# A list scheduler inside the kernel decides the order in which five engines get their instructions

## The chip, the cores and the metric

The kernel runs on one core of one Trainium2 chip. The metric is the device time of one execution in microseconds (us); lower is better. Before the change the median of three runs was 364.27 us (362.97 to 366.21). PE is TensorE, DVE is VectorE, ACT is ScalarE, POOL is GpSimd, SP is SyncE, which here only issues DMAs; PEld in the profiles is the loading of weights into PE. The order in which the program emits the instructions is what this change is about: an instruction that has to wait holds up those behind it on its engine, as a stall of 4.39 us on ScalarE further down shows.

## The reference, cut to what matters

Two stages follow each other. The first is attention over 4 batches x 8 heads x 768 positions x 64 dimensions, in which every query may look at only the 6 best of its 32-key chunks. "Best" is an upper bound, computed from the per-chunk minima and maxima of the keys. The second is a gated FFN over the 3072 resulting rows.

```python
k_min = np.min(k_chunks, axis=3)                # chunks of 32 keys
k_max = np.max(k_chunks, axis=3)
ub = np.sum(np.maximum(q * k_min, q * k_max), axis=-1)      # shapes cut
top_chunks = np.argsort(ub, axis=-1)[..., -top_k:]          # top_k = 6, causal
scores = scale * np.matmul(q, k.transpose(0, 1, 3, 2))
scores = np.where(sel & causal, scores, -1e9)
attn = softmax(scores) @ v                                  # written out in full there
# x: 3072 rows of 512, width of the FFN 1536
xn = x / rms(x) * rms_g
out = (silu(xn @ w_gate) * (xn @ w_val)) @ w_out
```

## The kernel before

The work falls into 12 blocks of 256 tokens. For each block and each group of four heads ("job") there is a preparation: transpose k and q (`kT`, `qT`), cast them (`kb`, `qb`), cast v (`VX`), place the chunk bounds (`KS`), compute the upper bounds on PE (`ub`), rank them and turn them into masks (`mt`, and `mo`, a copy of `mt` on the other half of the partitions). Then come the score units (`sc`, exponentials `pt`), the values (`avn`), the normalised rows (`xnat`, scaled `xs`, turned `tp`/`xsT`), and the FFN: six pairs of gate and value matmuls (`gp`, `vp`) and two projections (`op`) per block.

The values of a job are cast by GpSimd:

```python
def p_values(j):
    nc.gpsimd.tensor_copy(VX[j % KEEP_K][:, :, :, 0:D], st[j]["vraw"][:])
```

The order of all this is a fixed interleave, written by hand. The first two blocks have a script of their own (cut). After that a loop over the score units puts one slice of FFN and one step of preparation between the parts of a unit:

```python
for i in range(2, NU):
    ...
    if nxt:
        need(nxt)
        scores(nxt)
    sl = next_slice(i, 0)          # a gate/value pair or a projection, if due
    sl and sl.part()
    if nxt:
        exps(nxt, 0)
        triangle(nxt, 0)
    prep(0)                        # one step of a later job's preparation
    sl and sl.part()
    if nxt:
        exps(nxt, 1)
        triangle(nxt, 1)
    sl and sl.rest()
    run_later()
    ...
    values(u, 0, avn, [kg], pts)
    if last:
        normalise(u, 0, avn)
    prep(1)
    sl = next_slice(i, 1)
    sl and sl.rest()
    ...
```

The softmax here doesn't subtract the row's maximum and nothing guards it: scores larger than these inputs give would overflow.

## Time and profile before

| | before |
|---|---|
| median time | 364.27 us (3 runs) |
| span of the profiled run | 364.5 us |
| PE busy / idle | 316.9 / 47.6 us |
| mean granted clock of PE | 0.934 |
| first gate matmul of the FFN | 33.5 us |

These are lines of the profile's page: busy times by engine, then the lines of PE, VectorE and the clock that cut the span into 40 slices of 9.1 us (a digit is the busy share in tenths; `PEclk` is the granted clock in tenths), and the chain of work that ended last.

```profile
span 364.5 us, 11291 instructions
...
PE 316.9 (87%) x4565; PEld 230.6 (63%) x4588; DVE 233.5 (64%) x583; ACT 199.3 (55%) x321; POOL 197.1 (54%) x329
...
PE   8667987699779889899879889899799898998995
...
DVE  6676775657865875974875974876866946415240
...
PEclk9965998959996999999989989999989999999999
...
PE 56%; DVE 18%; DMA 8%; SPq 6%; ACT 5%; issue 5%; POOL 1%; DVEq 0%; POOLq 0%; ACTq 0%
...
```

PE is the engine that bounds the kernel, but it is not full in most slices, and its clock sags in the first third. The chain of waits goes through PE for 56% of the span and through VectorE for 18%. What PE waits for is in the view of waits (line, releaser, total us, times, longest):

```profile
...
PE sc L333 <- DVE mt L291: 11.8, 10, 2.1
PE tp L428 <- DVE xs L414: 6.3, 6, 2.8
PE avn L371 <- DVE xnat L386: 4.8, 6, 1.7
PE sc L333 <- DVE mo L297: 3.5, 10, 0.6
...
```

The next view gives the busy time of each engine in two stretches: up to the first gate matmul (at 33.5 us), then up to the last values of attention (at 328.6 us); the FFN that is left after that is not shown.

```profile
...
core 0: us, PE busy (x) PEld busy (x) DVE busy (x) ACT busy (x) POOL busy (x), PEclk, DMA share, GB/s
0.00:33.50 33.50, 23.12 (x246) 11.72 (x250) 21.90 (x66) 9.54 (x15) 19.13 (x45) 0.81 1.00 197
33.50:328.60 295.10, 263.18 (x4089) 196.72 (x4107) 200.91 (x502) 173.16 (x276) 163.22 (x270) 0.94 0.29 78
...
```

Read the last columns: the clock is 0.81 in the start and 0.94 in the long middle, and the DMA engines are full (share 1.00) only in the start. In the middle PE is idle for 295.1 - 263.2 = 31.9 us.

I also charged every matmul in the trace's records with the time until the next one starts, less the recorded idle time, and took off what the recorded half clock cost. That splits PE's time into real work at full clock, keep-warm matmuls (on zeros, to hold the clock up), clock loss, and idle. This split is worked out from the records of the profiled run, so its tenths are not to be pressed:

| before, us | real work | warm | clock loss | idle |
|---|---|---|---|---|
| 0 to 33.5 | 6.8 | 11.9 | 4.4 | 9.1 |
| 33.5 to 328.6 | 246.9 | 0 | 16.3 | 31.9 |
| 328.6 to 360.5 | 30.6 | 0 | 0 | 1.3 |

The 1.3 us before the first matmul and the last 4 us, for the final eviction and store, are outside the table. The profiled run was the slowest of the four of this kernel (366.21 us, clock 0.934); in the later rounds the clock of its runs is 0.934 to 0.950, with a median of 0.946. So some 4 us of the clock loss in this table may be this one run's: an estimate, (0.946 - 0.934) x 364.5.

### The profile page before, as it was taken

What the parts mean: (1) busy time and instruction counts of PE and PEld (TensorE: products, weight loads), DVE (VectorE), ACT (ScalarE), POOL (GpSimd) and SP (SyncE); (2) the same over time, 40 slices, a digit from 0 to 9 for tenths busy, and PEclk for the clock granted to TensorE, in tenths of its full rate; (3) what the DMA queues carried; (4) which work ended last, traced back from release to release, by engine and by line L of the source; (5) the groups of instructions that cost most, each with busy time, mean ns of one, the idle gap of its engine ahead of it and who ended that gap; (6) DMA issues with size and microseconds to landing.
All of it is one profiled execution on the core that took longest, in us unless ns stands there. A gap on an engine that the chain in (4) does not pass through costs nothing.

```text
span 364.5 us, 11291 instructions
## 1 busy us (share of the span) xinstructions
PE 316.9 (87%) x4565; PEld 230.6 (63%) x4588; DVE 233.5 (64%) x583; ACT 199.3 (55%) x321; POOL 197.1 (54%) x329
## 2 busy tenths in 40 slices
PE   8667987699779889899879889899799898998995
PEld 3334773478547657677756766777576675867682
DVE  6676775657865875974875974876866946415240
ACT  2340772537543754756554655775666475846361
POOL 6652592337844663763953752875763753336261
PEclk9965998959996999999989989999989999999999
DMA  6999954651242034125204204111001001010001
GB/s 178 191 198 241 220 148 134 174 131 43 66 141 70 20 88 121 42 74 147 72 18 147 64 27 146 45 39 67 3 2 59 2 3 59 2 46 17 30 31 58
DMA packets 43317, 30.63 MB, mean 84 GB/s; under 512 B 29440, under 2 KB 34048, under 8 KB 43264
## 3 DMA queue, kind: packets, MB, share of 16 engines
q1 hardware_dynamic: 38160, 24.66, 24.5%
q0 software_dynamic: 4720, 4.72, 7.9%
q8 instruction: 36, 0.59, 0.6%
q10 hardware_dynamic: 384, 0.52, 0.4%
q14 instruction: 17, 0.14, 0.1%
HBM read 28.31 MB, written 6.29 MB: 95 GB/s over the span
## 4 chain that ended last, share of the span: by engine, by line
PE 56%; DVE 18%; DMA 8%; SPq 6%; ACT 5%; issue 5%; POOL 1%; DVEq 0%; POOLq 0%; ACTq 0%
PE op L474 15%; PE gp L451 14%; PE vp L451 11%; DMA kraw<-in_k_dram 5%; PE ub L259 5%; PE avn L371 4%; SPq L88 4%; DVE tg L464 4%; PE sc L317 4%; ACT th L458 2%; DVE qT L197 2%; DVE xs L414 2%; PE sc L333 2%; DVE xnat L386 2%; DMA rmsg<-in_moe_rms_g_dram 2%
## 5 line engine op out<-in xcount | busy, mean ns | idle before, releaser
L468 POOL TENSOR_TENSOR hh<-tg,vs 128x512 bf16<-128x512 bf16 x72 | 83.0, 1153 | 70.6 <-ACT vs L461 55.5
L347 ACT ACTIVATE pt<-sc 128x768 bf16<-128x768 f32 (+1 forms) x96 | 85.6, 913 | 48.1 <-PE sc L333 48.0
L464 DVE SCALAR_TENSOR_TENSOR tg<-th,gp 128x512 bf16<-128x512 bf16 x72 | 49.2, 683 | 57.5 <-ACT th L458 55.7
L451 PE MATMUL gp<-xsT,wg 128*128 128x256 bf16 x576 | 80.0, 285 | 3.4 <-DVE xsT L430 2.0
L451 PE MATMUL vp<-xsT,wv 128*128 128x256 bf16 x576 | 79.6, 284 | 2.8 <-DVE tg L464 2.4
L474 PE MATMUL op<-wo,hh 128*128 128x512 bf16 x268 | 65.2, 387 | 2.0 <-issue 1.3
L451 PEld LDWEIGHTS <-wv 128*128 128x128 bf16 x576 | 58.7, 102 | 12.8 <-issue 3.7
L451 PEld LDWEIGHTS <-wg 128*128 128x128 bf16 x576 | 53.8, 101 | 15.4 <-issue 5.4
L458 ACT ACTIVATE th<-gp 128x512 bf16<-128x512 f32 x72 | 43.1, 598 | 30.3 <-PE gp L451 26.9
L461 ACT ACTIVATE vs<-vp 128x512 bf16<-128x512 f32 x72 | 43.2, 600 | 15.3 <-PE vp L451 13.8
L474 PEld LDWEIGHTS <-hh 128*128 128x128 bf16 x288 | 26.6, 99 | 33.3 <-issue 3.1
L481 ACT ACTIVATE osb<-op 128x512 f32<-128x512 f32 x24 | 14.3, 597 | 47.5 <-PE op L474 46.3
L371 PEld LDWEIGHTS <-pt 128*128 128x128 bf16 x672 | 31.0, 101 | 13.4 <-DVE xnat L386 6.5
L333 PE MATMUL sc<-mt,chunkrow 32*128 32x128 bf16 (+1 forms) x352 | 27.1, 213 | 11.8 <-DVE mt L291 11.8
L317 PE MATMUL sc<-qb,kb 32*128 32x256 bf16 (+1 forms) x768 | 36.0, 266 | 1.5 <-DVE ubn L270 1.5
L355 POOL TENSOR_SCALAR_AFFINE_SELECT pt<-pt 128x512 bf16<-128x512 bf16 x48 | 30.6, 640 | 9.0 <-ACT pt L347 7.8
L333 PEld LDWEIGHTS <-chunkrow 32*128 32x128 bf16 x704 | 20.3, 96 | 20.0 <-issue 18.9
L197 DVE STREAM_TRANSPOSE qT<-qraw 128x512 f32<-128x512 f32 x24 | 26.6, 1106 | 0.6
L270 DVE STREAM_TRANSPOSE ubn<-ub 128x256 f32<-128x256 f32 (+1 forms) x24 | 9.2, 381 | 27.5 <-PE ub L259 27.2
L197 DVE STREAM_TRANSPOSE kT<-kraw 128x512 f32<-128x512 f32 x24 | 26.5, 1104 | 0.1
L333 PE MATMUL sc<-mo,chunkrow 32*128 32x128 bf16 (+1 forms) x352 | 23.0, 214 | 3.5 <-DVE mo L297 3.5
L234 POOL TENSOR_SCALAR qraw<-qT 128x512 f32<-128x512 f32 (+1 forms) x24 | 12.5, 519 | 21.0 <-DVE qT L197 18.3
(138 smaller groups left out, 389.4 us busy)
## 6 DMA issues: line engine op xcount, KB each, us to landing
vraw<-in_v_dram SPq DMA_DIRECT2D x48, 128.0 KB, 2.9
out_dram<-osb SPq DMA_DIRECT2D x24, 256.0 KB, 2.1
kraw<-in_k_dram SPq DMA_DIRECT2D x92, 64.0 KB, 2.3
qraw<-in_q_dram SPq DMA_DIRECT2D x92, 64.0 KB, 2.0
wg<-in_moe_w_gate_dram POOLq DMA_DIRECT2D x3, 512.0 KB, 7.3
wv<-in_moe_w_val_dram POOLq DMA_DIRECT2D x3, 512.0 KB, 10.1
wo<-in_moe_w_out_dram POOLq DMA_DIRECT2D x1, 1536.0 KB, 19.3
kraw<-in_k_dram ACTq DMA_DIRECT2D x4, 64.0 KB, 2.4
```

Source lines behind the costliest of these rows:

```text
L197: nc.vector.transpose(out=st[j][nm + "T"].rearrange("p h (r j) -> p j h r", r=32, j=8), in_=st[j][nm + "raw"][:],)
L317: nc.tensor.matmul(sc[a // 2][:, a % 2, 256 * e:256 * e + BLK - q0], st[jk]["kb"][r, t, ks], st[jq]["qb"][r, t, q0:], start=(t == 0), stop ...
L333: nc.tensor.matmul(sc[a // 2][:, a % 2, 256 * e + lo - q0:256 * e + hi - q0], chunkrow[r, kr], mt[:, lo - m0 - C * w:w], start=False, stop ...
L347: nc.scalar.activation(out=pt[:, hs, 0:W], in_=u["sc"][hp][:, :, 0:W], func=ACT.Exp, scale=SCALE)
L355: nc.gpsimd.affine_select(out=dg, in_=dg, compare_op=ALU.is_ge, fill=0.0, base=0, pattern=[[0, 4], [1, P]], channel_multiplier=-1,)
L371: nc.tensor.matmul(avn[:, a, :], pts[kg][:, a, off:off + P], vext[:, e, a, :], start=(kb == 0 and a == 0), stop=(kb == nkb - 1 and a == 3) ...
L451: nc.tensor.matmul(ps[:, i * W:(i + 1) * W], w[:, g, ht * P:(ht + 1) * P], x[:, g, 0:W], start=(g == 0), stop=(g == NP - 1), skip_group_ch ...
L458: nc.scalar.activation(out=th[:], in_=gp[:], func=ACT.Tanh, scale=0.5)
L461: nc.scalar.activation(out=vs[:], in_=vp[:], func=ACT.Copy, scale=0.5)
L464: nc.vector.scalar_tensor_tensor(out=tg[:], in0=th[:], scalar=1.0, in1=gp[:], op0=ALU.add, op1=ALU.mult,)
L468: nc.gpsimd.tensor_tensor(out=hh[hp][:], in0=tg[:], in1=vs[:], op=ALU.mult)
L474: nc.tensor.matmul(op[:], hh[ht // K][:, o:o + P], wo[:, ht, :], start=(ht == 0), stop=(ht == NHT - 1),)
```

## The change

The intent is to replace the hand-made interleave by a schedule. Every piece of work becomes an `Op` with the engine (or engines) that may run it, a modelled duration in ns, a priority key, and its dependencies, among them the reuse of buffers and of PSUM banks. A list scheduler simulates the five engines with these durations: whichever engine can start something earliest takes, of the ops that are ready, the one with the lowest key. The instructions are then emitted in the order of the simulated start times. Nothing of this runs on the chip; only the order arrives there.

```diff
+def arrange(ops, banks, free):
+    ...
+    while len(done) < len(ops):
+        best = None
+        for e, cand in pool.items():
+            ...                                   # t: when its inputs and banks are there
+            at = max(free[e], min(t for t, _ in avail))
+            o = min((o for t, o in avail if t <= at), key=lambda o: (o.key, o.seq))
+            if best is None or at < best[0]:
+                best = (at, e, o)
+        at, e, o = best
+        o.eng, o.start, o.end = e, at, at + o.ns
+        free[e] = o.end
+        ...
+    done.sort(key=lambda o: (o.start, o.seq))
+    return done
```

Some of the ops with their durations and keys. `key` for attention is the number of the block; FFN of block c has the key c + 3.1, so attention runs up to three blocks ahead and the FFN fills what it leaves open:

```diff
+    o = add("SP", 1720.0, -1000.0 + n, lambda e, w, j=j, nm=nm: load(j, nm), lands=(740.0, 92.0))
+    o = add("SP", 860.0, -1000.0 + n, lambda e, w, j=j: load_v(j), lands=(1340.0, 20.0))
+    x["mt"] = add("DVE", 280.0 + 350.0 * f, key, lambda e, w, j=j: p_masks(j), x["lt"])
+    x["vc"] = add(("POOL", "ACT"), 590.0, key + 0.3, lambda e, w, j=j: p_values(j, e), load_of["v", j])
+    x["xs", s] = add("DVE", 290.0, key - 1, lambda e, w, tt=2 * blk + s: scale_x(tt), x["ri"])
+    y["g"] = add("PE", ns, key, ..., *xt, w_ops["wg", wi], pg, take=(("F", 1),))
+    ...
+    for o in arrange(ops, BANKS, free):
+        nwarm = 0
+        if o.eng == "PE":
+            gap = o.start - pe_free
+            pe_free = o.start + o.ns
+            if gap > 500.0:
+                nwarm = int(0.7 * gap / 216.0)     # warm matmuls in a planned gap
+        o.fn(o.eng, nwarm)
-    for i in range(2, NU):
-        ...                                       # the whole loop above goes
```

Other parts: the casts (`kb`, `qb`, `VX`) may go to ScalarE or GpSimd; `pt`, `xs` and `osb` have 6, 4 and 3 buffers instead of 5, 2 and 2; the mask rows are filled at first only as far as block 0 needs them. Arithmetic, shapes and bytes are the same.

## The prediction

> What bounds the kernel now. TensorE (PE), but it is not full. The page gives PE 316.9 us busy of 364.5 (87%), VectorE 233.5, ScalarE 199.3, GpSimd 197.1; the chain of work that ended last is 56% PE and 18% VectorE. So PE stands idle 47.6 us. The granted clock averages 0.93, about 24 us lost. Keep-warm matmuls take about 14 us. By stretches, the first 60 us lose most: PE idle 13.5 us, clock 0.61 to 0.92 between 10 and 60 us; the first gate matmul issues at 33.5 us. From 60 us on PE idles about 33 us (4 of them at the end), mostly waits of 1 to 3 us for VectorE (mt before the mask matmuls 11.8 us, xs before the transposes 6.3, xnat before avn 4.8), and clock dips cost about 15 us. The Trainium skill ("TensorE: Matmul & The Clock Gate", Part 1) says that an idle window halves the array's clock; the timeline agrees: after a wait of 2.15 us at 181.5 us a gate group took 1.89 us instead of 1.05.
>
> What the change does. Arithmetic and shapes stay. By the instruction order, PE gets the same real matmuls and 79 warm ones instead of 44, all but eight in the startup. The fixed interleave becomes a work-conserving list schedule: attention runs up to three blocks ahead, and the gate/value matmuls fill whatever would be a gap. In the emitted order only three planned PE gaps of over 0.5 us are left after the startup. Some casts may go to ScalarE, and pt, xs and osb have more buffers. The tail is now three whole blocks of FFN without attention, about 52 us of dense PE; the old tail shows such pairs at PE's pace (1.76 us; ScalarE 1.2, GpSimd 1.15).
>
> Cost, from full-clock intervals in the timeline: 72 gate/value pairs of 1.76 us = 127; 24 projections of about 2.6 = 62; 48 score units of 0.53 to 0.77 = 33; 24 bounds of 0.6 to 1.06 = 21; avn 23; transposes 8; with seams about 277 us of needed PE work. VectorE, by start-to-start intervals, needs about 215, so it can keep up.
> New time: first gate matmul at about 28 us (the block-0 chain loses the steps put into it; DMA, at a share of 1.0 to 1.2 from 10 to 40 us, still limits the weights), about 6 us of the work done by then; 271 us remaining; last eviction and store 4; leftover waits 8 to 15; cold clock 2 to 5. Sum 313 to 323; I take 316. Nearly all of the gain is on the critical path, since PE is that path: about 5 us from startup, 43 from fewer waits and clock dips later.
>
> What would show it. PE idle down from 47.6 to about 20 to 28 us; granted clock at 0.97 or more; first gate matmul before 30 us; PE's waits for mt and xs together under 6 us (now 18); VectorE nearly idle in the last 50 us.
>
> Against it. The order rests on modelled durations and engines run it in order, so a late load or a slow instruction stalls all behind it. Early weight loads may delay k and q of blocks 1 and 2, starving PE between 25 and 50 us. The two score banks are held by every unit until both exponentials end; if ScalarE runs late, attention loses its lead.
>
> Chances: faster by over 2% 0.95, within 2% 0.03, slower 0.02.

## More of the kernel before

The masks are made like this; the two copies at the end matter later:

```python
nc.vector.transpose(out=st[j]["mt"][:, :, 0:ni * CH], in_=...)     # cut
for R in range(2):
    C = 1 - R
    nc.vector.tensor_copy(
        st[j]["mo"][64 * R:64 * (R + 1), 0:ni * CH],
        st[j]["mt"][64 * C:64 * (C + 1), R, 0:ni * CH])
```

## The result, and the profile after

| | before | after |
|---|---|---|
| median time | 363.62 us (4 runs, 362.90 to 366.21) | **338.02 us** (4 runs, 336.88 to 338.60) |
| span of the profiled run | 364.5 us | 335.9 us |
| PE busy / idle | 316.9 / 47.6 us | 309.3 / 26.6 us |
| mean granted clock of PE | 0.934 | 0.977 |
| first gate matmul | 33.5 us | 34.8 us |

Ratios here are the mean time of one kernel's runs over that of the other's of the same rounds, so not quite the ratio of the medians quoted: 0.928, with a 95% interval of 0.9225 to 0.9335. Executions over 1.5% slower than the fastest of the same kernel are left out of the means. The change made the kernel 7.2% faster. The prediction's sum gave 313 to 323 us and it took 316; the direction was right, the size was not, by 22 us.

The same lines of the page after:

```profile
span 335.9 us, 11381 instructions
...
PE 309.3 (92%) x4623; PEld 222.6 (66%) x4623; DVE 232.9 (69%) x589; ACT 211.9 (63%) x347; POOL 184.4 (55%) x308
...
PE   8969999967989989978999899999999999999994
...
DVE  7988799956798999999999999653523352413140
...
PEclk9998999998779999999999999999999999999998
...
PE 49%; DVE 20%; DMA 10%; SPq 10%; issue 4%; ACT 4%; POOL 2%; DVEq 0%; ACTq 0%; POOLq 0%
...
```

PE is at 9 tenths in most slices, VectorE is at 9 tenths from the 14th to the 25th slice (of 8.4 us), and the last fifth (from 267.1 of 335.9 us) has no attention. Note the chain: SPq, the queue that issues loads, grew from 6 to 10% and DMA from 8 to 10%. The chain now runs more through loads.

PE's waits after:

```profile
...
PE avn L506 <- DVE xnat L521: 4.7, 3, 2.2
PE ub L387 <- ACT pt L484: 3.2, 1, 3.2
PE avn L506 <- POOL pt L490: 2.6, 4, 1.8
...
PE tp L557 <- DVE xs L545: 2.0, 4, 0.7
...
```

The waits for `mt` (11.8 us before) are gone to 0.3 and those for `xs` are 2.0. New at the second place is a wait that `ub` spends on `pt`, an output of ScalarE, once, for 3.2 us; and one of `avn` on the `pt` of GpSimd.

The stretches after (the middle is split in three; the columns are those of before):

```profile
...
0.00:34.80 34.80, 28.55 (x344) 14.44 (x345) 29.94 (x92) 13.03 (x20) 20.25 (x54) 0.95 0.96 187
34.80:90.00 55.20, 48.66 (x884) 37.59 (x883) 43.11 (x106) 39.19 (x65) 32.51 (x61) 0.94 0.73 172
90.00:180.00 90.00, 83.51 (x1541) 61.20 (x1538) 86.53 (x228) 63.32 (x102) 57.59 (x103) 0.98 0.43 113
180.00:267.10 87.10, 84.82 (x1378) 62.31 (x1375) 53.69 (x137) 62.44 (x103) 45.48 (x66) 1.00 0.07 23
267.10:331.50 64.40, 63.72 (x493) 47.10 (x490) 19.64 (x29) 33.36 (x58) 28.58 (x26) 1.00 0.09 34
...
```

VectorE is busy 86.53 of the 90 us from 90 to 180, so in that stretch it is nearly as full as PE. The tail, from 267.1 us on, is 64.4 us of dense PE, as planned. And PE's split as above:

| after, us | real work | warm | clock loss | idle |
|---|---|---|---|---|
| 0 to 34.8 | 8.2 | 18.6 | 1.7 | 5.0 |
| 34.8 to 267.1 | 210.0 | 2.0 | 5.0 | 15.3 |
| 267.1 to 331.5 | 63.8 | 0 | 0 | 0.7 |

Compared with the table of before: the middle and the tail lost 17.2 us of idle and 11.3 us of clock loss and gained 2.0 of warm matmuls. Real work is 2.3 us less, which is about the error of such a split. So the gain is fewer gaps and less half clock in the middle (of the half clock some 4 us less than the tables say, by the estimate above). In the start, idle and clock loss fell by 6.8 us, but 6.7 us of warm matmuls came in their place: waiting dressed as work. The time of the first gate matmul, less the work done by then, is 26.6 us after and 26.7 before. Nothing was gained there. The table of stretches shows one thing that stood in the way: VectorE was busy 29.94 us before the first gate matmul, and 21.90 in the old order. The schedule put more work of block 1 beside block 0, not less: 4 mask transposes (`mt`) begin before the first gate matmul, where the old order had the 2 of block 0.

### Where the order stalls

The emitted order has three planned PE gaps of over half a microsecond after the start. The trace has 15.3 us of idle in the middle. Where does the biggest idle stretch come from? PE's timeline (start, us, instruction, and in brackets the idle time before it with its releaser):

```profile
...
68.87 1.04 PE L577 MATMUL gp<-xsT,wg 128*128 128x256 bf16 x8
73.13 0.21 PE L387 MATMUL ub<-late,ident 64*64 64x32 bf16 x4 [3.22 <-ACT pt L484]
...
74.93 1.92 PE L577 MATMUL gp<-xsT,wg 128*128 128x256 bf16 x8
...
```

`ub` needs a score bank, and the bank comes free when ScalarE has done the exponentials. ScalarE's timeline in the same stretch:

```profile
...
71.02 0.63 ACT L328 ACTIVATE VX_187<-vraw 128x512 bf16<-128x512 f32 x1 [4.39 <-DMA vraw<-in_v_dram]
...
72.07 1.00 ACT L484 ACTIVATE pt<-sc 128x1024 bf16<-128x1024 f32 x1
...
```

The exponential at 72.07 us stood behind a cast of v, `VX_187`, which waited 4.39 us for its load. PE's wait is thus a wait for a DMA, through ScalarE's queue. In the PE timeline, the gate group at 68.87 us took 1.04 us and the one at 74.93 us 1.92 us: the gap was followed by half clock. The Trainium skill ("TensorE: Matmul & The Clock Gate", "Architectural detail") says of the queues "ACT/DVE are strict FIFO; GPSIMD is per-Q7 strict FIFO"; the trace agrees, since the scores had been done by 68.1 us and their exponential did not pass the cast. GpSimd has the same thing a little later. These are the longest waits of the casts for v:

```profile
...
POOL VX_178 L330 <- DMA vraw<-in_v_dram: 6.0, 1, 6.0
...
ACT VX_187 L328 <- DMA vraw<-in_v_dram: 4.4, 1, 4.4
...
```

Why is the load late? The plan has 1.72 us for SyncE to issue the four DMAs of a k or q load. The DMA queue's timeline shows what it was:

```profile
...
19.17 6.89 SPq L216 DMA_DIRECT2D kraw<-in_k_dram  x4
26.11 9.05 SPq L216 DMA_DIRECT2D qraw<-in_q_dram  x4
35.33 1.70 SPq L216 DMA_DIRECT2D kraw<-in_k_dram  x4
...
```

Two issues took 6.89 and 9.05 us, while the weights were coming in (the view of stretches gives the DMA engines a share of 1.22 from 20 to 35 us), and the next one 1.70 (those up to 50 us then 2.8 to 3.8). In this queue each of the 257 issues begins only after the one before has ended, so all later loads start late, and the plan does not know it.

### VectorE's durations

Three groups of VectorE instructions, first of the kernel before, then after (the columns behind the bar are total us and mean ns of one):

```profile
...
L414 DVE TENSOR_SCALAR xs<-xnat,ri_all 128x512 bf16<-128x512 bf16 x24 | 10.4, 473 | 4.0 <-POOL ri_all L408 4.0
...
L297 DVE COPY mo<-mt 64x128 bf16<-64x128 bf16 x32 | 8.4, 263 | 0.8
...
L291 DVE STREAM_TRANSPOSE mt<-mk 128x256 bf16<-128x256 bf16 x16 | 7.1, 445 | 0.5
...
```

```profile
...
L545 DVE TENSOR_SCALAR xs<-xnat,ri_all 128x512 bf16<-128x512 bf16 x24 | 12.9, 553 | 2.6 <-POOL ri_all L541 2.3
L433 DVE COPY mo<-mt 64x128 bf16<-64x128 bf16 x32 | 12.2, 380 | 0.8
...
L427 DVE STREAM_TRANSPOSE mt<-mk 128x256 bf16<-128x256 bf16 x16 | 6.9, 432 | 0.1
...
```

The plan has 290 ns for an `xs`; it took 473 ns before and 553 after. For `mt` with its two copies it has 630 ns at full width; 432 + 2 x 380 = 1192 ns is what it took after. The copies even got longer than before. In the records, a `mo` copy during which GpSimd was idle took 0.18 us in both kernels, and one during which GpSimd was working 0.46 us before and 0.44 after (0.89 in the 7 cases beside the product `hh`). What the change moved is how often the two meet: 17 of 48 copies before, 33 of 48 after. In both traces together, 14 copies began while `hh` was running, and each ended 0.03 to 0.05 us after `hh` did; two that began just before an `hh` took 0.17 and 0.19 us. So beside `hh` the copy waits for its end. The Trainium skill ("SBUF — State Buffer", "SBUF: two separate sides") says that VectorE and GpSimd share a port pair as "an exclusive lock, not a bandwidth split", for some VectorE instructions; these numbers agree with it, though no run here took GpSimd away.

### The profile page after: what moved, and what is told of

The parts are those of the page before. It is cut to its first block, busy times and chain, and to the rows that moved or that the text cites. A ratio compares the mean times of both kernels' runs of the same rounds, so it can differ in the third digit from the quotient of the medians.

```text
span 335.9 us, 11381 instructions
## 1 busy us (share of the span) xinstructions
PE 309.3 (92%) x4623; PEld 222.6 (66%) x4623; DVE 232.9 (69%) x589; ACT 211.9 (63%) x347; POOL 184.4 (55%) x308
## 4 chain that ended last, share of the span: by engine, by line
PE 49%; DVE 20%; DMA 10%; SPq 10%; issue 4%; ACT 4%; POOL 2%; DVEq 0%; ACTq 0%; POOLq 0%
PE op L607 14%; PE vp L577 11%; PE gp L577 11%; SPq L216 8%; DMA vraw<-in_v_dram 5%; PE avn L506 4%; PE ub L387 3%; DVE tg L593 3%; PE sc L456 3%; DMA kraw<-in_k_dram 3%; DMA qraw<-in_q_dram 3%; DVE xs L545 2%; DVE kT L321 2%; SPq L228 2%; DVE qT L321 2%
## 5 line engine op out<-in xcount | busy, mean ns | idle before, releaser
L577 PE MATMUL gp<-xsT,wg 128*128 128x256 bf16 x576 | 75.7, 275 | 0.8 <-DVE xsT L563 0.8
L577 PE MATMUL vp<-xsT,wv 128*128 128x256 bf16 x576 | 75.0, 273 | 0.9 <-DVE tg L593 0.8
L607 PE MATMUL op<-wo,hh 128*128 128x512 bf16 x288 | 66.3, 385 | 0.2 <-DVE tg L593 0.2
L577 PEld LDWEIGHTS <-wv 128*128 128x128 bf16 x576 | 54.1, 98 | 9.1 <-issue 2.1
L506 PEld LDWEIGHTS <-pt 128*128 128x128 bf16 x672 | 26.9, 99 | 13.0 <-DVE xnat L521 4.5
L456 PE MATMUL sc<-qb,kb 32*128 32x256 bf16 (+1 forms) x768 | 33.5, 259 | 1.9 <-DVE ubn L397 1.4
L531 ACT ACTIVATE junk<-xnat 128x512 bf16<-128x512 bf16 x24 | 15.2, 632 | 21.5 <-DVE xnat L521 21.5
L472 PE MATMUL sc<-mt,chunkrow 32*128 32x128 bf16 (+1 forms) x352 | 24.8, 208 | 0.3 <-DVE mt L427 0.3
L456 PEld LDWEIGHTS <-kb 32*128 32x128 bf16 x768 | 13.9, 93 | 12.8 <-issue 11.9
L521 DVE TENSOR_TENSOR xnat<-avn,rden 128x256 bf16<-128x256 f32 x48 | 20.4, 425 | 1.8
## 6 DMA issues: line engine op xcount, KB each, us to landing
wg<-in_moe_w_gate_dram POOLq DMA_DIRECT2D x3, 512.0 KB, 11.8
```

The costliest lines, as they stand in the source:

```text
L456: nc.tensor.matmul(sc[a // 2][:, a % 2, 256 * e:256 * e + BLK - q0], st[jk]["kb"][r, t, ks], st[jq]["qb"][r, t, q0:], start=(t == 0), stop ...
L472: nc.tensor.matmul(sc[a // 2][:, a % 2, 256 * e + lo - q0:256 * e + hi - q0], chunkrow[r, kr], mt[:, lo - m0 - C * w:w], start=False, stop ...
L506: nc.tensor.matmul(o[:, a, :], us[kg]["pt"][:, a, off:off + P], vext[:, e, a, :], start=(kb == 0 and a == 0), stop=(kb == nkb - 1 and a == 3),
L577: nc.tensor.matmul(ps[:, i * W:(i + 1) * W], w[:, g, ht * P:(ht + 1) * P], xsT[c][:, g, 0:W], start=(g == 0), stop=(g == NP - 1), skip_gro ...
L607: nc.tensor.matmul(op[:], sl[c, ht // K, "hh"][:, o:o + P], wo[:, ht, :], start=(ht == 0), stop=(ht == NHT - 1),)
```

## The experiments

After the result, the question was why 338 and not 316. The theories were:

1. **Late loads.** Casts of v, placed early in ScalarE's and GpSimd's queues by a plan that believes the loads on time, stall everything behind them.
2. **VectorE.** The plan has VectorE's durations too short, so the order is wrong where VectorE is nearly full.
3. **Startup.** The chain of block 0 through all engines, cut open by other work, is too long.
4. **Rivals**: the gain comes from the extra buffers and not from the order; the order is a matter of luck that any nudge changes; warm matmuls cost time; the durations in the plan don't matter at all.

Where a text shortens a theory to a letter, S is the startup; what each expected is repeated after it. All kernels below computed the right result. Each was timed in three rounds beside the kernel before, whose median in the four sets was 364.4 to 364.8 us, so medians can be set beside the 338.02 us of the changed kernel. Edits are to the changed kernel unless "before" is named.

### x_beforebufs: the buffers alone (kernel before)

```diff
-    ptp = ... tile_pool(name="ptp", bufs=5)
+    ptp = ... tile_pool(name="ptp", bufs=6)
-    xs.append(ev.tile([P, DM], BF16, name="xs"))
+    xs.append(ev.tile([P, DM], BF16, name="xs", bufs=4))
-    osb = ffn.tile([P, DM], FP32, name="osb", bufs=2)
+    osb = ffn.tile([P, DM], FP32, name="osb", bufs=3)
```

> The kernel before with the changed kernel's deeper buffers alone (pt 6, xs 4, osb 3), old order. Theory (the gain is the order): 362 to 365 us. Rival (the gain is the buffers): 350 us or less.

Measured: 364.65 us, ratio to before 1.0003 (0.9962 to 1.0045). The buffers alone give nothing in the old order. The gain belongs to the rest of the change: mostly the order (x_flat below loses 19.6 us by the order alone), with the later mask rows (about 4 us, x_rows below). What the casts gain by being allowed on ScalarE was not tested apart.

### x_flat: the same scheduler with meaningless durations

```diff
+    if "SP" not in self.engs:
+        ns = {"PE": 1000.0, "DVE": 600.0, "ACT": 700.0, "POOL": 700.0}[self.engs[0]]
     self.ns, self.key, self.fn = ns, key, fn
```

> The changed kernel with all durations in the scheduler's model the same per engine (PE 1000, VectorE 600, ScalarE and GpSimd 700 ns). If the gain comes from calibrated durations: 350 us or more. If it comes from emitting op by op whatever is ready, in any sane order: 338 to 346 us.

Measured: 357.66 us (356.85 to 358.22), ratio 0.9809 (0.9767 to 0.9852). Expected was 350 or more if the durations matter, and it came. With the same keys, dependencies and buffers, but one duration per engine, 19.6 of the 25.6 us are lost. So what the scheduler is told of the durations is most of what it is worth, and errors in them are a plausible place for the missing 22 us.

### x_placebo: is it luck?

```diff
-            ns = 870.0                             # a gate group
+            ns = 885.0
-            o = add("PE", 2690.0, ...project...)
+            o = add("PE", 2600.0, ...project...)
```

> The changed kernel with two durations of the scheduler's model a little different (gate 885 instead of 870 ns, projection 2600 instead of 2690), which gives another order after the first 45 us but changes no idea. It measures how much the luck of an order is worth: 338 plus or minus 3 us. If it lies outside that, single orders can't be compared at the level of 1%.

Measured: 338.76 us (337.40 to 340.08), ratio 0.9287. A nudge of the plan by 2 to 3% that corrects nothing gives another order (by the traces, on all engines from about 47 us on) and moves the time by less than 1 us. This is one draw only; x_nolead below, also another order, gives 339.18 us. So steps of 5 us below are well above what a mere change of order did here, steps of 1 to 2 us are not.

### x_loads: tell the plan how long the issues took

```diff
-            o = add("SP", 1720.0, -1000.0 + n, ...load...)
+            ns = {("k", 4): 6900.0, ("q", 4): 9100.0, ("q", 5): 3100.0, ("k", 6): 3800.0,
+                  ("q", 6): 2800.0, ("k", 8): 2700.0}.get((nm, j), 1900.0)
+            o = add("SP", ns, -1000.0 + n, ...load...)
```

> The changed kernel, only the schedule's model told how long the issues of six loads took in its own trace (6.9 and 9.1 us for k and q of job 4 instead of 1.72, and so on). Theory L (loads land later than the plan thinks, so casts of v stand at the head of ScalarE's and GpSimd's queues and stall all behind them): PE gaps plus clock loss between 60 and 100 us fall from about 12 us to under 4, time 327 to 332 us. Rival P (what is left is PE's own work and luck of the order): 336 to 340 us.

Measured: 336.02 us (334.32 to 337.89), ratio 0.923. Expected was 327 to 332. A miss. The stalls at 70 and 82 us went, but a new one of 2.96 us came at 86 us: PE waits for `hh` of GpSimd, which stands behind an op that waits 4.54 us for ScalarE, where two casts of v wait 2.17 and 2.42 us for their loads. The casts of v on GpSimd waited 15.9 us in total over 7 cases. Feeding the plan the times of one trace did not hold; the likely reason, not tested apart, is that the new order changes when loads are asked for.

### x_vdep: don't put the cast where it can stall

```diff
+        if kg == 0 and jq >= 2:
+            J[jq]["vc"].deps.append(x["sc"])       # after the first scores of its own group
```

The cast of v is needed only by `avn`, after the scores. The plan put it as early as its load was believed to land. The edit keeps it back, so that the load has time; it adds a dependency and takes no wait away.

> The changed kernel with one more rule in the scheduler: the cast of v of a job (2 and later) waits until the first scores of its own group are out, so that no cast stands in ScalarE's or GpSimd's queue long before its load. Theory L: the waits of casts for v (about 20 us in the changed kernel, 6.0, 4.4, 3.2, 2.7 and 2.3 the longest) fall under 4 us, the PE gaps of 3.2 and 1.8 us at 70 and 82 us and the half-clock stretches after them go, 328 to 333 us. Rival P (what is left is PE's own work and the luck of an order): 336 to 340.

Measured: 332.44 us (331.72 to 333.76), ratio 0.9126 (0.9077 to 0.9175). Expected under late loads was 328 to 333. What is left of the casts' waits for v on all engines is one line:

```profile
...
ACT VX L328 <- DMA vraw<-in_v_dram: 0.6, 1, 0.6
...
```

From over 20 us to 0.6. The stalls of the first theory cost 5.6 us of time. PE's idle and clock loss in the middle fell from 20.3 to 15.9 us, and the FFN's tail from 63.8 to 63.6, so most of the gain is where it was expected. The theory holds, for a quarter of the miss.

### x_onedma: fewer DMAs for k and q

```diff
+        if j >= 2:
+            nc.sync.dma_start(
+                out=t[:].rearrange("p j h d -> p (j h d)"),
+                in_=src[b, 4 * g:4 * g + 4, BLK * m:BLK * (m + 1), :].rearrange(
+                    "a (r j) d -> a r (j d)", r=32, j=8),
+            )
```

(The loop over the four DMAs stays for jobs 0 and 1; cut.) One DMA of 256 KB instead of four of 64 KB, with the order of all else unchanged, as the traces of VectorE and ScalarE confirm. I took the long issues for a cost per DMA.

> The changed kernel with the same emission order on PE, DVE, ACT and POOL, but each k or q load of jobs 2 and later is one DMA of 256 KB and not four of 64 KB, so SyncE's queue has about a quarter of the issue work. Theory L with SyncE's issue as the reason for the lateness: loads come earlier, the stalls at 67 to 71 us (ScalarE) and 75 to 81 us (GpSimd) go, 327 to 332 us. If the lateness is only bandwidth (weights fill the DMA engines from 20 to 45 us): at most 3 us better, 335 to 338. Rival P: 338.

Measured: 364.33 us (363.61 to 365.61), ratio 0.9993. Expected was 327 to 332, or 335 to 338 if issues don't matter; it lost the whole gain. The stretch from 35 to 60 us, first of the changed kernel, then of this one:

```profile
...
35.00:60.00 25.00, 24.28 (x408) 17.87 (x405) 22.58 (x55) 19.65 (x34) 14.76 (x24) 1.00 0.89 190
...
```

```profile
...
35.00:60.00 25.00, 18.47 (x307) 13.26 (x302) 13.53 (x42) 14.02 (x23) 8.63 (x14) 0.99 0.56 117
...
```

The DMA engines are at 0.56 instead of 0.89 and move 117 GB/s instead of 190. Then the load queue of this experiment:

```profile
...
37.40 0.73 SPq L216 DMA_DIRECT2D qraw<-in_q_dram  x1
38.22 20.77 SPq L234 DMA_DIRECT2D vraw<-in_v_dram  x4
59.09 2.67 SPq L216 DMA_DIRECT2D kraw<-in_k_dram  x1
...
```

The issue of v now takes 20.77 us, behind the slow loads. The Trainium skill ("DMA: Bandwidth & Descriptors", "Rules for kernel authors") says that the number of engines of a DMA follows from the slowest dimension of its access patterns, so that "an outermost dim of size c < 16 [...] confines the whole DMA to at most c engines". The source here has the outermost dimension 4. The trace agrees: from 38 to 58 us, of the 2 KB packets of the load queue 5 or more were in flight together for under 1% of the time, in the changed kernel for half of it and up to 18. The same list also says to coalesce many small transfers into one; here that advice alone cost 26 us. For the argument the run shows something else: the identical order with later loads is 26 us slower. The order has no slack against loads as late as these.

### x_nowarm: without the warm matmuls of the planned gaps

```diff
-                nwarm = int(0.7 * gap / 216.0)
+                nwarm = 0
```

> The changed kernel with the same order but none of the 49 keep-warm matmuls after the first 30. If they are filler off the critical path: within 1.5 us of 338, with PE idle up by about 18 us in the startup and the first gate matmul still at 34 to 35 us. If they hold the clock up where it matters: clock loss before the first gate up from 1.7 us to 4 or more and the first gate 1 to 3 us later. If, at half clock, they stand in the way (four took 1.9 us before the bounds of job 2): first gate up to 1 us earlier.

Measured: 338.35 us (337.49 to 340.03), ratio 0.9282. No difference in the total. The start did what was expected if the warm matmuls hold the clock up: the first gate matmul came at 36.7 us instead of 34.8, and the start's clock loss rose from 1.7 to 5.4 us. But the stall at 69.9 us was gone, and the one of 1.82 us at 81.9 us became one of 4.03 us at 80.7 us, again behind a cast that waits for v (6.81 us). So 1.9 us in the start did not show in the total; that the loads set the pace up to 90 us would explain it and is not tested further.

### x_rows: the mask rows whole at the start

```diff
-    fill_rows(0, BLK, Q0, BLK)
+    fill_rows(0, S, 0, S)
-    spread_rows(0, BLK, Q0, BLK)
+    spread_rows(0, S, 0, S)
-    rows = add("POOL", 2600.0, 0.5, ...)           # the later part, and what waits for it
-    rows = add("DVE", 1700.0, 0.5, ...)
```

> The changed kernel with the mask rows built whole at the start, as in the kernel before (no 2.8 us of copies on VectorE at 23 to 26 us, between the first values and their normalising). Theory S (the order of VectorE's queue holds up the first block): first gate at 31 to 33 us instead of 34.8; the time falls by as much only if the loads, which bind at 60 to 90 us, allow it: 334 to 338. Rival: first gate stays at 34 to 35 (DMA binds).

Measured: 342.11 us (341.94 to 343.24), ratio 0.9386. I expected the first gate matmul at 31 to 33 us, because the later part of the rows would no longer stand in block 0's chain. It came at 39.2 us. In this form the startup theory fell; putting off part of the rows, as the change does, is worth about 4 us.

### x_block0: keep block 1 out of block 0's way (on top of x_vdep)

```diff
+    for o in (J[2]["kT"], J[2]["qT"], J[3]["kT"], J[3]["qT"], rows):
+        o.deps.append(J[1]["mt"])
```

> x_vdep with the preparation of block 1 on VectorE (transposes of jobs 2 and 3, the second part of the mask rows) held back until the masks of job 1 are made. Theory S (VectorE's queue, filled with work for block 1, delays block 0): first gate at 30 to 32.5 us instead of 35.5; total 329 to 332 if nothing is lost later. Rival (the startup's chain is DMA or latency): first gate stays at 34 to 36.

Measured: 333.40 us (332.57 to 335.14), ratio 0.9156, against 332.44 for x_vdep. The first gate matmul moved from 35.5 to 33.1 us and the total did not follow: real PE work done by then fell from 8.6 to 7.2 us, and later there were 2.1 us more of warm matmuls. What block 0 gains, block 1 seems to pay. I found no order that brings the first gate matmul to the predicted 28 us.

### x_nolead: less lead for attention

```diff
-        key = b0 + n - 1 + 3.1
+        key = b0 + n - 1 + 1.1
```

> The changed kernel with the FFN's keys two blocks earlier (block number plus 1.1, not plus 3.1): the FFN is preferred to attention of the block after next, so attention cannot run three blocks ahead. If the lead is what fills PE's gaps: PE gaps after the first gate rise from 16 to 25 us or more, 343 to 352 us, with a tail of one or two blocks. If it is not (any work-conserving order will do): 335 to 341.

Measured: 339.18 us (338.30 to 341.62), ratio 0.931. The edit was meant to shorten the lead and hardly did: the tail still had 55.7 us of real FFN work, as many as x_placebo with the keys unchanged. For the lead this is inconclusive. It shows only that this shift of the keys hardly matters; that readiness decides nearly every choice is my guess at why.

### x_hardlead: less lead, by a dependency

```diff
+    for i, u in enumerate(units):
+        b, qt, g, kg = u["key"]
+        blk = b * NBLK + qt
+        if g == 0 and kg == 0 and blk >= 2:
+            U[i]["sc"].deps += F[blk - 2]["g"][:4]
```

> The changed kernel with a hard limit on the lead: the first scores of a block wait until the gates of the first half of the FFN two blocks back are out. The tail after the last avn shrinks from about four blocks' FFN (64 us) to little over one. If attention's lead is a reserve that fills PE's gaps: gaps after the first gate over 25 us, 343 to 352 us. If VectorE's saturation during the lead is what hurts: fewer gaps, 330 to 336. If neither: 336 to 341.

Measured: median 345.86 us; the three fast runs were 344.42, 344.90 and 346.83, and the ratio of these is 0.9483. The run that was profiled (350.28 us) was a slow one, so its profile is used for one thing alone: the tail is now 24.4 us of real work instead of 63.8, so the lead is really shorter. Expected was 343 to 352 if the lead is a reserve, and it came: with the short lead the kernel is about 7 us slower, so the long tail is not a loss. That the FFN that is pushed back fills gaps of attention is the likely reason; the gaps themselves were not measured in a fast run.

### x_cal: VectorE's durations as measured (on top of x_vdep)

```diff
-        x["mt"] = add("DVE", 280.0 + 350.0 * f, ...)
+        x["mt"] = add("DVE", 540.0 + 680.0 * f, ...)
-        x["lt"] = add("DVE", 90.0 + 300.0 * f, ...)
+        x["lt"] = add("DVE", 130.0 + 360.0 * f, ...)
-            x["xs", s] = add("DVE", 290.0, ...)
+            x["xs", s] = add("DVE", 480.0, ...)
-            y["st"] = add("DVE", 610.0, ...)
+            y["st"] = add("DVE", 635.0, ...)
```

> x_vdep with VectorE's durations in the scheduler's model as its trace shows them on average (masks 1.2 instead of 0.63 us, scaling 0.48 instead of 0.29, comparison 0.49 instead of 0.39, tg 0.635 instead of 0.61). Theory D (VectorE, 29 of 30 us busy from 120 to 210 us, runs longer than planned, because its copies wait for GpSimd, and the order slips there by about 9 us): PE gaps after the first gate from 14 to about 10 us, 328 to 331 us. Rival (the order is good enough, only VectorE's work itself costs): 331 to 335.

Measured: 326.23 us (325.96 to 326.43), ratio 0.8952 (0.8922 to 0.8982). Expected was 328 to 331, or 331 to 335 if VectorE's durations don't matter; it came below both. Four durations in a plan are worth 6.2 us beyond x_vdep. Idle in the middle fell from 14.4 to 5.3 us. And VectorE did not have to get emptier for it: from 90 to 180 us it is busy 84.30 us (86.07 in x_vdep), while PE rises from 80.50 to 86.45.

### x_cal_only: the durations without the held-back cast

> The changed kernel with only VectorE's durations corrected in the model, without the rule for the casts of v. If late loads and VectorE's durations are separate causes: about 6 us above x_cal, 330 to 334 us, with waits of the casts for their loads of 5 us and more. If VectorE's durations alone were the cause (the casts stall only because the plan is off): 326 to 328.

Measured: 328.51 us (327.29 to 328.91), ratio 0.9014 (0.8988 to 0.9040). If the two causes were separate, 330 to 334 was expected, and if it was VectorE alone, 326 to 328; it fell between. So the causes seem to overlap: 5.6 us for the cast alone, 9.5 for the durations alone, 11.8 for both, 3.3 less than the sum. The casts still wait for v:

```profile
...
POOL VX L330 <- DMA vraw<-in_v_dram: 17.3, 7, 4.1
...
ACT VX L328 <- DMA vraw<-in_v_dram: 11.2, 7, 6.5
...
```

Those are 28.5 us of stalls, more than in the changed kernel, at a lower total. A stall on ScalarE or GpSimd costs what it costs PE, and with the better order elsewhere more of them were covered.

### x_moact: take load from VectorE (on top of x_vdep)

```diff
-            nc.vector.tensor_copy(
-                st[j]["mo"][64 * R:64 * (R + 1), 0:ni * CH],
-                st[j]["mt"][64 * C:64 * (C + 1), R, 0:ni * CH])
+            nc.scalar.activation(
+                out=st[j]["mo"][64 * R:64 * (R + 1), 0:ni * CH],
+                in_=st[j]["mt"][64 * C:64 * (C + 1), R, 0:ni * CH], func=ACT.Copy)
-        x["mt"] = add("DVE", 280.0 + 350.0 * f, ...)
+        x["mt"] = add("DVE", 90.0 + 320.0 * f, ...)
+        x["mo"] = add("ACT", 500.0, key, lambda e, w, j=j: p_other(j), x["mt"])
         ...                                       # cut: the scores now wait for mo, not mt
```

> x_vdep with the two mo copies of each job on ScalarE instead of VectorE, where they took 0.42 us each when GpSimd was busy and 0.19 when it was idle. VectorE's busy time falls by about 17 us, ScalarE's rises by about 12. Theory D: VectorE binds the stage from 90 to 210 us, so attention and PE get on faster there: 326 to 330 us. Rival (PE's work binds, VectorE only fills its slack): 331 to 334.

Measured: 324.10 us (323.35 to 325.35), ratio 0.8898 (0.8862 to 0.8934). Expected was 326 to 330. The stretch from 90 to 180 us, first of x_vdep, then of this kernel:

```profile
...
90.00:180.00 90.00, 80.50 (x1541) 60.69 (x1543) 86.07 (x216) 65.54 (x110) 55.23 (x99) 0.99 0.39 99
...
```

```profile
...
90.00:180.00 90.00, 87.80 (x1611) 65.34 (x1610) 78.96 (x195) 75.00 (x136) 59.79 (x107) 1.00 0.42 114
...
```

VectorE falls from 86.07 to 78.96 us in these 90 us, and PE rises from 80.50 to 87.80. That fits the second theory, seen from the other side: give VectorE room instead of telling the plan that it has none. But the edit does both. With the copies gone, the plan has 410 ns for the masks at full width, and the trace 432; the two copies have 500 in the plan and 2 x 308 in the trace. So what the room is worth apart from the truer plan is not shown, and x_cal got nearly as far (326.23 us) without giving room.

### x_before_moact: the same edit without a scheduler (kernel before)

> The kernel before with its mo copies on ScalarE. It has waits of 15.3 us of PE for mt and mo, of which mo 3.5. If VectorE's queue held PE up in the old order as well: 355 to 361 us. If the old order itself is the limit: 362 to 366.

Measured: 368.25 us (366.66 to 368.88), ratio 1.0104 (1.0072 to 1.0136). I expected a gain, 355 to 361 us, or little, 362 to 366, and got a loss of 1%. PE now waits for the copies on ScalarE, where it had waited 3.5 us for VectorE:

```profile
...
PE sc L333 <- ACT mo L297: 9.7, 12, 2.3
...
```

In the fixed order the copy stands behind exponentials and row sums in ScalarE's queue. In x_moact, where the scheduler places it, PE waits only 0.5 us for it. The edit's worth depends on who places it.

### x_moact_cal: the copies on ScalarE and the measured durations

> All three finds together: casts of v bound to their group's scores, mo copies on ScalarE, and VectorE's remaining durations in the model as measured. Gaps, clock loss and warm matmuls between first gate and last avn were 22.3 us in the changed kernel, 9.1 with the calibrated model, 7.7 with mo on ScalarE. If the two are independent: 5 us left, 320 to 323 us. If they remove the same waits: 323 to 326.

x_moact, with the durations of `lt`, `xs` and `st` as in x_cal. Measured: 323.21 us (322.90 to 323.65), ratio 0.8875 (0.8854 to 0.8896). Expected was 320 to 323 if the two add up, 323 to 326 if not. They don't: with the copies on ScalarE, the other durations bring 0.9 us, no more than a mere change of order does. This is the best version, and it beats both kernels, by 11.2% and by 4.4% (323.21 against 338.02). Two lines of its page:

```profile
span 321.9 us, 11374 instructions
...
PE 303.2 (94%) x4618; PEld 220.6 (69%) x4618; DVE 219.3 (68%) x541; ACT 223.8 (70%) x395; POOL 184.2 (57%) x308
...
```

PE's idle is 18.7 us, 4.4 of them in the middle. What stays is 281.0 us of real work, a start of 36.4 us of which 7.7 are real work, and the end.

## Why the prediction was right or wrong

The sum that gave 316 can be set beside what the trace shows, term by term. The first column is the prediction's text, rearranged: 28 - 6 for the start, 271 + 6 for the work, and 316 leaves 13 for waits and cold clock.

| term, us | predicted | measured | off by |
|---|---|---|---|
| first gate matmul, less PE work done by then | 22 | 34.8 - 8.2 = 26.6 | 4.6 |
| PE work needed | 277 | 282.0 | 5.0 |
| leftover waits, cold clock and warm matmuls after that | 13 | 15.3 + 5.0 + 2.0 + 0.7 = 23.0 | 10.0 |
| last eviction and store | 4 | 4.4 | 0.4 |
| median time over the span of the profiled run | 0 | 338.0 - 335.9 = 2.1 | 2.1 |
| sum | 316 | 338.1 | 22.1 |

- **Mechanism: right.** PE was the bound and is it still. PE's idle fell from 47.6 to 26.6 us (predicted 20 to 28), the clock rose to 0.977 (predicted 0.97 or more), PE's waits for `mt` and `xs` fell to 0.3 + 2.0 us (predicted under 6), VectorE is busy 12.4 of the last 50 us (predicted nearly idle, so this one came in part). These signs came, and the time did not. They count what vanished; none counts what PE needs. The one other sign, a first gate matmul before 30 us, did not come.
- **"8 to 15" of leftover waits and "2 to 5" of cold clock: the step that failed most.** The prediction read three planned gaps in the emitted order and took the plan nearly at its word. It named the danger ("a late load or a slow instruction stalls all behind it") and gave it no size. Both came. Taking the late casts out was worth 5.6 us, telling the plan VectorE's true durations 9.5, both 11.8, and taking the copies off VectorE with both 14.8. In the last of these kernels, x_moact_cal, the term measures 8.2 us instead of 23.0, less than the 13 allowed for; the sum of that kernel is 28.7 for the start, 281.0 of work, 8.2 and 4.0 for the end, together its span of 321.9. So these edits together account for the 10.0 us of the term. And the prediction had the evidence: the plan's 290 ns for `xs` and 630 for the masks stood in the changed kernel, and 473 and 445 + 2 x 263 = 971 ns in the profile of before.
- **"VectorE [...] needs about 215, so it can keep up": an average that hid the stage.** The attention that runs ahead brings VectorE's work forward: 86.53 busy of the 90 us from 90 to 180, and 19.64 of the 64.4 in the tail. It could keep up only where the plan knew how full it was: x_cal has PE at 86.45 there beside a VectorE at 84.30, x_vdep at 80.50 beside 86.07.
- **"Early weight loads may delay k and q of blocks 1 and 2, starving PE between 25 and 50 us": right cause, wrong victim.** The issues of k and q were delayed in just that stretch, but PE was not starved there; it was v, behind them in the queue, that came late, and the longest stalls of its casts (2.7, 4.4 and 6.0 us) ended at 69 to 81 us.
- **"First gate matmul at about 28 us": wrong.** It came at 34.8, and x_block0, the best attempt at it, brought 33.1 with nothing to show for it in the total. The step "the block-0 chain loses the steps put into it" is the one that failed here: other steps took their place, and VectorE had 29.94 us of work before the first gate matmul instead of 21.90. Holding block 1's back (x_block0) gained 2.4 of the 7.5 us by which x_vdep lay above 28; what holds the rest is open. The startup gave nothing of the 5 us expected of it.
- **"About 277 us of needed PE work": too small.** The same accounting gives 284.3 us before and 282.0 after. The prediction added up clean stretches of each kind. By the same accounting of the changed kernel's trace, the gate/value pairs take 130.9 us, not 127 (1.82 us each, not 1.76), scores 34.7, bounds 22.3, values 24.3 and projections 63.0, each 1 to 2 us more than predicted; the transposes take 6.7 instead of 8. The trace of before could have told: charge every matmul up to the next one, and don't add up the best.
- **"Three whole blocks of FFN [...] about 52 us of dense PE":** 64.4 us long, with 0.7 us of idle: 24 gate/value pairs and 8 projections, which is four blocks. The reserve is longer than I said; x_hardlead shows that cutting it costs 7 us.

What stays open: how the 22 us fall on the terms is an accounting of one profiled run, and only the third term was tested by removing causes. For the start, I can say that three edits did not shorten it usefully, not that it can't be shortened.

## What to carry to other kernels

In this kernel the static schedule was worth what its durations were worth: the same scheduler with flat durations kept 6 of 26 us, and correcting four of them gave 9.5 more, so compare each modelled duration with the trace before believing a planned gap. An op that waits for a DMA had better not be placed as soon as the plan says that the data has landed, but later, nearer to its consumer: here that was worth 5.6 us. And when a bound engine's work is estimated, charge it from start to start over the whole trace, with warm matmuls and half clock taken apart, because "busy" counts both as work.

## What the Trainium skill lacked or had wrong

- "TensorE: Matmul & The Clock Gate", Part 1, has the clock fall "after ≥1 idle window (~3.4µs)". The windows are as it says: in the trace after, half clock came in stretches of 3.41 us, at 23.54, 74.74, 84.98 and 95.22 us, all multiples of 3.41 us apart. But the windows before them were idle for only 2.35, 1.79, 2.17 and 1.43 us, worked out from the records (the prediction's own example, a wait of 2.15 us, is also shorter than an idle window). In all 18 profiles here, every such window at full clock with more than 1.82 us of recorded idle was followed by half clock, the first and last of a run left out; of those with 1.05 to 1.82 us some were and some were not. Its rule of "No PE-idle gaps >~3µs" (section "Why this matters for your kernels") is thus too lax: a gap of 1.82 us, with 0.35 us more in the same window, cost a window here.
- "DMA: Bandwidth & Descriptors", "Rules for kernel authors", gives coalescing as a rule and, elsewhere in the list, the rule on the outermost dimension. Coalescing four 64 KB loads into one with the outermost dimension 4 took the kernel from 338.0 to 364.3 us; the first rule does not name the second.
- No page that I read gives the time of an issue on SyncE under full DMA engines: four DMAs of a load took 1.70 us, and 6.89 and 9.05 us while the weights came in.
- "SBUF — State Buffer", "SBUF: two separate sides", tells of the lock between VectorE and GpSimd without a number for small copies: a 64-partition bf16 copy took 0.18 us with GpSimd idle and 0.44 us on average with GpSimd working, 0.89 us where it began during the product `hh` (1.16 us).
